# A third product of a Strassen-Winograd gate-and-up stage divided once more, with its results assembled in PSUM banks, in a GEGLU kernel on one core

## The chip, the core and the metric

The kernel runs on one core of a Trainium2 chip. Its engines work side by side, each through a queue of its own in program order: TensorE (PE: matmuls, and PEld: the loads of their stationary operand), VectorE (DVE), ScalarE (ACT), GpSimd (POOL), and SyncE (SP), which here only issues DMAs. They wait for each other by semaphores. The metric is the device time of one execution in microseconds (us), the median of several runs.

## The reference

```python
B, S, Dm, Df = 1, 2048, 1024, 3584          # x, w_gate, w_up, w_down in bfloat16
g = einsum("bsd,df->bsf", x, w_gate)
u = einsum("bsd,df->bsf", x, w_up)
h = gelu(g) * u                              # tanh form
return einsum("bsf,fd->bsd", h, w_down)
```

Here 2048 tokens with 1024 features go through two matrices to 3584 hidden features, one half passes a GELU and is multiplied by the other, and a third matrix leads back to 1024.

## The kernel before

**Winograd's form.** Each of the three matrix products is done by Strassen's method in Winograd's form: both factors are cut into quarters, a few sums of quarters are made (S1 to S4 of the weights, T1 to T4 of the inputs), and seven products of half the size, P1 to P7, take the place of eight. For gate and up, one *unit* (of 14, NU) is 256 columns of w_gate and w_up; the inputs come in two halves of 1024 tokens, p = 0 and 1, and a product of one half is four matmuls of 128x128 by 128x512. Units 0 to 3 run first, one half of the tokens at a time (`unit`, line 241). Units 4 to 13 run with both halves together (`joint`, line 299): four products P1 (raw weights, bf16), P6 = S2 T2, P5 = S1 T1, P2 (raw, bf16) and P7 = S3 T3 with four matmuls for each half and each of gate and up. Two of the seven products are divided once more there, P3 = S4 B22 (T named "tb") and P4 = A22 T4: such a product of 16 matmuls is itself done in Winograd's form, by seven half products of two matmuls each (`half`, line 295), 14 in all.

**PSUM.** There are eight banks of 128x512 float32. A unit has four banks E[p][i] (half p; i = 0 gate, 1 up), in which P1, P6 and P5 are added up one on the other, and four banks F, of which z and y hold the parts of the divided products and two the raw P2. At the end of a unit E and F change places. Intermediate states are copied out of the banks by ACT (`snap`, line 104: p1, u2, v, zz) and added by DVE (`dve`, line 88); GELU is ACT's, and `times` (line 205) makes the product h = gelu(g) u on DVE and has SP store it in DRAM (hd).

**Sums.** POOL makes the sums of weights (`sums_s`, line 163: S1 to S4 from 128x512 operands) for the next unit, the quarter sums of the divided products (`split_sums`, line 191: four operations of 128x256), the sums of the down weights (`keep_whole`, line 425: three operations of 128x512 for each of 14 chunks j, two such chunks in most units from 5 on), which SP stores in DRAM (td, line 432) for the down products, and, once, the differences of the inputs for the divided products (`split_b`, line 282: eight operations each for "tb" and "t4", lines 994 and 998, at the end of unit 3). T of the first half of the tokens lies in 20 slots, T of the second in rooms that later hold h.

**Slots.** Most small tiles share one pool of 54 slots of 2 KB a partition (kpool, line 64). A tile gets a slot that is free or will be; its first writer then waits for the last reader of the tile that was there. Sums of down weights had a pool of their own (mpool: 6 KB, one buffer), as had the products h on their way out (spool: 4 buffers of 1 KB).

**Order.** PE, DVE, POOL and SP run in the order in which the program names their instructions (line 58), ACT too in this stage (line 944). In `joint` the order is that of its statements; sums, loads and stores are asked for at seven places in it, by name ("p6", "p5", "p3", "p2", "p7", "p4", "end"; `joint_work`, line 885). The last product of a unit is finished during the next one (`rest`, line 395).

**Down products.** After unit 13, `down` (line 625) computes the output for each half of the tokens, from h and from the stored sums of down weights, which it loads again (`load12`, line 438). `inner_product` (line 578) belongs to the last half.

Of the kernel before, what the change touches and what calls it, by code (L numbers as in the profile page):

```python
# [10 lines left out]
def kernel(  # L11
# [35 lines left out]
    JOINT = 4  # L47
    H, Q, R2 = NJ // 2, N // 2, range(2)
    SLOTS = 54
# [10 lines left out]
    mpool = ctx.enter_context(tc.tile_pool(name="m", bufs=1))  # L60
# [4 lines left out]
    spool = ctx.enter_context(tc.tile_pool(name="s", bufs=4))  # L65
# [125 lines left out]
    def split_sums(a):  # L191
        a11, a12, a21, a22 = quarters(a)
        s12, s34 = [slot([P, 2, 2, P], f32r, "s") for _ in range(2)]
        pool(s12[:, 0], a21, a22, ADD)
        pool(s12[:, 1], s12[:, 0], a11, SUB)
        pool(s34[:, 0], a11, a21, SUB)
        pool(s34[:, 1], a12, s12[:, 1], SUB)
        return s12[:, 0], s12[:, 1], s34[:, 0], s34[:, 1]
# [6 lines left out]
    def times(p, fb, c, g, u):  # L205
        if (p, fb // 2) == (0, NU - 1) and h[1][c] is not None:
            dve(h[1][c][:, fb % NJ], g, u, MUL)
            return
        last = fb // 2 == NU - 1
        st = slot([P, N], bf16, "h") if last else spool.tile([P, N], bf16, name="h")  # L210
        dve(st, g, u, MUL)
        nc.sync.dma_start(out=hd[p, fb // NJ, c][:, fb % NJ], in_=st)  # L212
# [81 lines left out]

    def half(ps, lhs, rhs, fresh=False):
        for k in range(2):
            matmul(ps, lhs[:, k], rhs[k], fresh and k == 0, k == 1)

    def joint(u, E, F, todo, c21):
        GU = range(2)  # L300
        w, s = ws[u], ss[u]

        def copied(ps, *args):
            half(ps, *args)
            return snap(ps, "zz")

        def onto(t, ps):
            dve(t, ps, t, ADD)

        def gelu_of(t):  # L310
            nc.scalar.activation(t, t, ACT.Gelu_apprx_tanh)
            return t

        p1, u2, v = [[[None, None], [None, None]] for _ in range(3)]
        spread = (0, 1), (1, 0), (0, 0), (1, 1)
        for n, (p, i) in enumerate(spread):
            product(E[p][i], w[i][0][:, :, :P], XT[p, 0][:KH], True)
            p1[p][i] = snap(E[p][i], "p1")
            c21(n)
        todo("p6")  # L320
        s2 = s.pop("s2")
        for n, (p, i) in enumerate(spread):
            product(E[p][i], s2[i], T[p]["t2"], False)
            u2[p][i] = snap(E[p][i], "u2")
            c21(4 + n)
        todo("p5")
        z, y = F[0]
        s1 = s.pop("s1")
        a11, a12, a21, a22 = quarters(s["s4"])
        n1, n2, n3, n4 = ns["tb"]  # L330
        q1, q2, q3, q4 = sums.pop((u, "tb"))
        for p in range(2):
            for i in GU:
                product(E[p][i], s1[i], T[p]["t1"], False)
                v[p][i] = snap(E[p][i], "v")
            if p == 0:
                z1 = copied(z, a11, T[0]["tb"][:2], True)
                for i in GU:
                    nc.scalar.copy(out=F[1][i], in_=p1[1][i])
        todo("p3")  # L340
        z6 = copied(z, q2, n2)
        half(E[0][0], a12, T[0]["tb"][2:])
        half(y, q1, n1, True)
        onto(z1, E[0][0])
        half(E[0][1], a22, n4)
        onto(z6, y)
        z7 = copied(z, q3, n3)
        half(E[1][0], q4, T[1]["tb"][2:])
        ga = gelu_of(z1)
        onto(z6, E[1][0])  # L350
        dve(E[0][1], E[0][1], z7, ADD)
        onto(z7, y)
        times(0, 2 * u, 1, ga, E[0][1])
        dve(E[1][1], E[1][1], z7, ADD)
        gb = gelu_of(z6)
        todo("p2")
        for i in GU:
            product(F[1][i], w[i][1][:, :, :P], XT[1, 0][KH:], False)
        times(1, 2 * u, 1, gb, E[1][1])
        raw_second(F[0], 0, w)  # L360
        hb = gelu(F[1][0])
        onto(p1[0][0], F[0][0])
        dve(F[0][1], F[0][1], p1[0][1], ADD)
        times(1, 2 * u, 0, hb, F[1][1])
        ha = gelu_of(p1[0][0])
        todo("p7")
        s3 = s.pop("s3")
        n1, n2, n3, n4 = ns["t4"]
        q1, q2, q3, q4 = sums.pop((u, "t4"))
        sg, sh = sums.pop((u, "sa"))  # L370
        for i in GU:
            product(E[0][i], s3[i], T[0]["t3"], True)
        times(0, 2 * u, 0, ha, F[0][1])
        z1 = copied(z, sg[:, :2], T[0]["t4"][:2], True)
        for i in GU:
            product(E[1][i], s3[i], T[1]["t3"], True)
        onto(v[0][0], E[0][0])
        dve(F[1][0], E[0][1], v[0][1], ADD)
        onto(v[1][0], E[1][0])
        dve(F[1][1], E[1][1], v[1][1], ADD)  # L380
        todo("p4")
        z6 = copied(z, q2, n2)
        half(y, q1, n1, True)
        y5 = snap(y, "zz")
        ha = gelu_of(v[0][0])
        half(E[0][0], sg[:, 2:], T[0]["t4"][2:])
        half(E[0][1], sh, n4)
        z7 = copied(z, q3, n3)
        half(E[1][0], q4, T[1]["t4"][2:])
        hb = gelu_of(v[1][0])  # L390
        times(0, 2 * u + 1, 1, ha, F[1][0])
        times(1, 2 * u + 1, 1, hb, F[1][1])
        todo("end")

        def rest(part):
            if part == 0:
                dve(E[0][0], E[0][0], u2[0][0], ADD)
                onto(z1, E[0][0])
                for a in (u2[0][1], z7):
                    dve(E[0][1], E[0][1], a, ADD)  # L400
                for a in (u2[1][0], y5):
                    dve(E[1][0], E[1][0], a, ADD)
                onto(z6, E[1][0])
            if part == 3:
                times(0, 2 * u + 1, 0, gelu_of(z1), E[0][1])
                for a in (u2[1][1], z7, y5):
                    dve(E[1][1], E[1][1], a, ADD)
            if part == 7:
                times(1, 2 * u + 1, 0, gelu_of(z6), E[1][1])

        return rest
# [13 lines left out]
    def keep_whole(j):  # L425
        ra, rb = wraw.pop(j)
        m = made[j] = mpool.tile([P, 3, N], f32r, name="m")
        pool(m[:, 0], ra[:, N:], ra[:, :N], SUB)
        pool(m[:, 1], rb[:, N:], m[:, 0], SUB)
        pool(m[:, 2], rb[:, :N], m[:, 1], SUB)  # L430

    def store_made(j):
        nc.sync.dma_start(out=td[:, j], in_=made[j][:, :3].bitcast(f32))
# [138 lines left out]
    def store(ip, c, i, dc, put):  # L572
        st = slot([P, N], bf16, "st") if (c, dc) == (1, 0) else spool.tile([P, N], bf16, name="h")
        put(st)
        r0 = (2 * ip + c) * N + i * P
        nc.sync.dma_start(out=out2[r0 : r0 + P, dc * N : (dc + 1) * N], in_=st)

    def inner_product(ip, e, c, ss):
        zz = [mpool.tile([P, 3, N], f32, name="m")[:, :2], wpool.tile([P, 2, N], f32, name="w")]
# [238 lines left out]
    order = ["t2"] * KH + ["t1"] * KH + ["tb"] * KH + ["n"] * 2 + ["t3"] * KH + ["t4"] * KH + ["n"] * 6  # L818
# [8 lines left out]
    def more_room():  # L827
        extra = wpool.tile([P, KH, N], f32r, name="w")
        spots["n"][2:2] = [extra[:, k] for k in range(KH)]
# [23 lines left out]
    def at_p5(n):  # L853
# [19 lines left out]
        elif n == 6:  # L873
            new_s(JOINT, "s3", "s4")

    keeps = {}
    for j in range(NJ):
        n = 3 + j
        keeps[JOINT + n // 2, ("p2", "p3")[n % 2]] = j

# [4 lines left out]
    def joint_work(u, what):  # L885
        if what == "p6":
            if u in (JOINT, JOINT + 1):
                load_next(u + 1)
            if (u, "p3") in keeps:
                fetch_wd(keeps[u, "p3"])  # L890
            if u > JOINT:
                new_s(u, "s3")
        if what == "p5":
            if (u, "p2") in keeps:
                keep_whole(keeps[u, "p2"])
            sums[u, "t4"] = split_sums([loaded(u)[i][1][:, :, P:] for i in range(2)])
        if what == "p3" and (u, "p2") in keeps:
            store_made(keeps[u, "p2"])
        if what == "p2":
            if (u, "p3") in keeps:  # L900
                keep_whole(keeps[u, "p3"])
            halves = sums_s(loaded(u), pool)["how"]
            sums[u, "sa"] = halves["sg"](None), halves["sh"](None)
            if u + 1 < NU:
                new_s(u + 1, "s1", "s2")
        if what == "p7":
            if (u, "p3") in keeps:
                store_made(keeps[u, "p3"])
            ws.pop(u)
            if u % 2 == 0 and u > JOINT:  # L910
                load_next(u + 2)
            if u + 1 < NU:
                new_s(u + 1, "s4")
# [157 lines left out]
```

## Time and profile before

| what | us |
|---|---|
| median of 3 runs (lowest, highest) | 532.36 (532.31, 532.40) |
| the profiled execution | 532.63 |
| its span, first to last instruction | 530.8 |
| units 4 to 13, PE's first matmul of unit 4 to the first of the down products | 108.98 to 352.69 |
| one joint unit | 24.3 |
| the two down products | 352.69 to 530.8 |

The page's first part gives the busy time of each engine as a share of the span. The second cuts the span in 40 slices of 13.3 us, each digit the busy share of one engine in tenths. The windows view gives the same for chosen stretches. The chain of waits starts from the last instruction and goes back to whatever released each piece of work. The timeline lists instructions in order of time; several of one kind in a row are one line, marked xN.

### The profile page before, as it was taken

Reading aid. Unit: us, or ns where it says so; the run is one execution under the profiler, and the core shown is the slowest. Engines: PE = TensorE matmul, PEld = TensorE weight load, DVE = VectorE, ACT = ScalarE, POOL = GpSimd, SP = SyncE. Lnnn points to the kernel's source line nnn. Section 1 sums busy time; section 2 is a strip of 40 time slices with the busy share of each in tenths; the row PEclk is TensorE's granted clock in tenths of the full one; section 3 lists DMA queues with packets and bytes.
Section 4 is the critical chain, followed back from the end, with each engine's and each line's share of the span. In section 5 each row is a group of like instructions: output and inputs, shape, how many; then the busy total and the mean of one; then the engine's idle time right before and its main releaser. Section 6 shows DMA issues by size and latency. Waiting matters only on the chain.

```text
span 530.8 us, 7711 instructions
## 1 busy us (share of the span) xinstructions
PE 524.2 (99%) x2380; PEld 373.5 (70%) x2411; DVE 367.5 (69%) x568; ACT 274.9 (52%) x497; POOL 306.0 (58%) x311
## 2 busy tenths in 40 slices
PE   9999999999999999999999999999999999999997
PEld 5568686876767677777777676764688885488887
DVE  2984636427687878787876878788599336768933
ACT  2555655555857585666768576832126501133340
POOL 1179899899986999799779799200000000000495
PEclk9999999999999999999999999999999999999999
DMA  9687541331346754574738453699986999982851
GB/s 247 158 190 154 126 129 49 110 109 41 106 159 195 223 191 163 205 228 143 252 127 253 160 159 118 193 389 413 382 267 205 384 411 380 395 276 87 260 159 61
DMA packets 103513, 109.57 MB, mean 206 GB/s; under 512 B 19376, under 2 KB 84656, under 8 KB 103472
## 3 DMA queue, kind: packets, MB, share of 16 engines
q1 hardware_dynamic: 103472, 109.08, 63.4%
q8 instruction: 19, 0.31, 0.2%
q14 instruction: 22, 0.18, 0.1%
HBM read 76.28 MB, written 29.62 MB: 200 GB/s over the span
## 4 chain that ended last, share of the span: by engine, by line
PE 90%; POOL 6%; DMA 2%; issue 1%; SPq 0%; DVE 0%; POOLq 0%; DVEq 0%
PE bank L110 90%; POOL h L92 3%; POOL s L92 2%; DMA w<-in_w_up_dram 1%; POOL w L92 1%; DMA xn<-in_x_dram 1%; SPq L723 0%; DVE h L89 0%; DVE st L89 0%; PE bank L730 0%; SPq L131 0%; SPq L212 0%; POOLq L92 0%; DVEq L89 0%
## 5 line engine op out<-in xcount | busy, mean ns | idle before, releaser
L110 PE MATMUL bank<-h,s 128*128 128x512 f32 x508 | 127.7, 390 | 0.2 <-POOL s L92 0.2
L92 POOL TENSOR_TENSOR q<-q 128x256 fp32r<-128x256 f32 x28 | 25.5, 943 | 164.3 <-DMA q<-td 163.7
L110 PEld LDWEIGHTS bank<-h,s 128*128 128x128 f32 x508 | 95.2, 188 | 20.8 <-POOL s L92 0.6
L110 PE MATMUL bank<-xT,w 128*128 128x512 bf16 (+1 forms) x448 | 101.0, 375 | 1.5
L92 POOL TENSOR_TENSOR s<-w 128x512 fp32r<-128x512 bf16 (+1 forms) x82 | 85.1, 1055 | 12.4 <-DMA w<-in_w_gate_dram 11.8
L110 PEld LDWEIGHTS <-w 128*128 128x128 bf16 x504 | 47.3, 98 | 58.5 <-issue 5.8
L110 PE MATMUL bank<-t,s 128*128 128x512 f32 x312 | 83.1, 406 | 0.0
L89 DVE TENSOR_TENSOR zz<-bank,zz 128x512 f32<-128x512 f32 x60 | 40.5, 689 | 41.9 <-PE bank L110 28.5
L110 PEld LDWEIGHTS bank<-t,s 128*128 128x128 f32 x312 | 57.9, 188 | 15.6 <-ACT u L106 2.3
L110 PE MATMUL bank<-q 128*128 128x512 f32 x272 | 66.9, 390 | 0.0
L110 PEld LDWEIGHTS bank<-q 128*128 128x128 f32 x272 | 51.1, 188 | 10.7
L106 ACT COPY zz<-bank 128x512 f32<-128x512 f32 x70 | 40.5, 592 | 33.8 <-PE bank L110 29.9
L106 ACT COPY p<-bank 128x512 f32<-128x512 f32 x76 | 43.6, 588 | 20.3 <-PE bank L110 20.0
L89 DVE TENSOR_TENSOR q<-h,h 128x512 fp32r<-128x512 bf16 x56 | 38.3, 683 | 15.2 <-DMA h<-hd 12.4
L106 ACT COPY u<-bank 128x512 f32<-128x512 f32 x62 | 35.8, 589 | 23.5 <-PE bank L110 23.5
L89 DVE TENSOR_TENSOR bank<-bank,zz 128x512 f32<-128x512 f32 x60 | 41.8, 697 | 1.4
L92 POOL TENSOR_TENSOR s<-s,w 128x512 fp32r<-128x512 f32 (+1 forms) x40 | 41.2, 1046 | 0.8
L92 POOL TENSOR_TENSOR s<-w,s 128x512 fp32r<-128x512 bf16 (+1 forms) x40 | 41.4, 1051 | 0.0
L110 PEld LDWEIGHTS <-h 128*128 128x128 bf16 x224 | 21.7, 98 | 26.7 <-issue 0.5
L101 ACT CAST tb<-raw 128x512 fp32r<-128x512 bf16 x28 | 17.4, 627 | 44.4 <-PE bank L110 21.1
L110 PE MATMUL bank<-raw,h 128*128 128x512 bf16 x156 | 34.8, 379 | 0.2
L92 POOL TENSOR_TENSOR m<-raw,m 128x512 fp32r<-128x512 bf16 x28 | 32.9, 1175 | 2.2
(102 smaller groups left out, 772.6 us busy)
## 6 DMA issues: line engine op xcount, KB each, us to landing
raw<-in_w_down_dram SPq DMA_DIRECT2D x72, 256.0 KB, 4.3
q<-td SPq DMA_DIRECT2D x68, 256.0 KB, 5.3
hd<-h SPq DMA_DIRECT2D x110, 128.0 KB, 1.7
td<-m SPq DMA_DIRECT2D x14, 768.0 KB, 3.4
h<-hd SPq DMA_DIRECT2D x18, 512.0 KB, 6.9
h<-hd SPq DMA_DIRECT2D x6, 768.0 KB, 8.5
w<-in_w_gate_dram SPq DMA_DIRECT2D x8, 512.0 KB, 5.3
w<-in_w_up_dram SPq DMA_DIRECT2D x8, 512.0 KB, 6.5
```

The lines of the kernel that those rows point to most:

```text
L89: nc.vector.tensor_tensor(out=out, in0=a, in1=b, op=op)
L92: nc.gpsimd.tensor_tensor(out=out, in0=a, in1=b, op=op)
L101: nc.scalar.copy(out=t, in_=src)
L106: nc.scalar.copy(out=t, in_=ps)
L110: nc.tensor.matmul(ps, lhsT=lhs, rhs=rhs, start=start, stop=stop, skip_group_check=True)
```

## The change

In units 5 to 13 the product S3 T3 is divided too, by the same seven half products, H1 to H7 in the new code; unit 4 keeps it whole. Its results are not added up from copies in SBUF: three copies on ACT (e00, e10, e01) put the common part of z into banks E, on which the remaining half products are then accumulated, and two additions on DVE (e11, e10y) add the part y5. So the sum v + S3 T3 of the up half stays in SBUF (v01, v11), and its product with the GELU (m22a, m22b) reads two tiles in SBUF, where it read one in SBUF and one bank.

The statements of `joint` become named steps (`joint_ops`), and one table, SEQUENCE, gives their order for every engine: P, X, H, K, S, G are steps on PE; a leading minus marks steps that finish the unit before; @ marks places where sums, loads and stores are asked for. Half products of "tb" are X1 to X7, those of "t4" K1 to K7, the raw P2 of the two halves S0, S1 and G0, G1.

POOL makes the quarter sums of S3 in addition, in two parts of two operations, as now for "tb" and "t4" too. The differences of T3 are made by DVE (three), POOL (three, in unit 4, and two in unit 5); those of T4 are made by DVE in unit 4, no longer by POOL at the end of unit 3. S3 of unit 4 is made within that unit.

The pools for the sums of down weights and for the products h are gone, and the slots are 59. The sums of one j are three tiles stored by three DMAs. Their units are listed in KEEPS: one j in units 5, 6, 8, 10 and 12, two in 7, 9 and 11, three in 13; those of j = 4, 5, 6, made in unit 13, stay in their slots for the down products and two thirds of them are not loaded again.

```diff
+    DIVIDED7 = 5
+    STAY = 4, 5, 6
+    KEEPS = [(u, n) for u in range(5, 14) for n in range({7: 2, 9: 2, 11: 2, 13: 3}.get(u, 1))]
-    SLOTS = 54
+    SLOTS = 59
...
-    def split_sums(a):
+    def split_sums(a, part, before=None):
         a11, a12, a21, a22 = quarters(a)
...
+        t = slot([P, 2, 2, P], f32r, "s")
+        if part == 0:
+            pool(t[:, 0], a21, a22, ADD)
+            pool(t[:, 1], t[:, 0], a11, SUB)
+        else:
+            pool(t[:, 0], a11, a21, SUB)
+            pool(t[:, 1], a12, before[1], SUB)
+        return t[:, 0], t[:, 1]
...
+    def split_b3(part, eng=pool):
+        n = ns.setdefault("t3", [[], [], [], []])
+        for k in range(2):
+            b11, b12, b21, b22 = [T[p]["t3"][h + k] for h in (0, 2) for p in range(2)]
+            if part == k:
+                n1, n2, n4 = [slot([P, N], f32r, "n") for _ in range(3)]
+                eng(n1, b12, b11, SUB)
+                eng(n2, b22, n1, SUB)
+                eng(n4, b21, n2, SUB)
...
+            if part == 2:
+                eng(b12, b22, b12, SUB)
...
+    SEQUENCE = (
+        "@start -a00u P100 -a10u P101 @tb.0 -a00z P111 -m22a p101 @tb.1 -a01u P110 p100 -v11+ "
+        "-g21a P601 -a01z @keep p110 P600 -a11u -hb2 X1 u201 -m21a P610 u200 -m22b xz1 X5 -a10y "
+        "P501 p111 -a10z @s3 u210 X6 -a11z @store P500 v01 -a11y xz6 S0 -g21b x6y X7 @t3.0 v00 "
+        "-m21b P510 sg c11a xz7 X2 X4 v10 @t3.1 P611 x00 f0 x01 ha H1 @t4.0 X3 u211 x7y S1 ga x10 "
+        "@s1 H5 e00 m12a P511 @free gb c11b y5 H6 m11a H2 v11 K1 @t4.1 e10 x11 G0 kz1 v00+ H7 f1 "
+        "H3 m12b K6 @late e01 @s2 e11 G1 ha2 e10y kz6 H4 K5 v10+ sh K2 hb v01+ @s4 K7 ky5 K3 m11b "
+        "K4 kz7 @end "
+    ).split()
...
+        def inner(letter, left, tname, z, y):
...
+                out, a, b = [
+                    (z, a11, b11), (E[0][0], a12, b21), (E[1][0], q4, b22), (E[0][1], a22, n4),
+                    (y, q1, n1), (z, q2, n2), (z, q3, n3),
+                ][n - 1]
+                half(out, a, b, n in (1, 5))
...
+        if u < DIVIDED7:
+            for name in ("H1", "H5", "H6", "H7", "e00", "e10", "e01", "y5", "e11", "e10y"):
+                ops[name] = lambda: None
+            for name, outs in (("H2", PI[:1]), ("H3", PI[2:3]), ("H4", PI[1::2])):
+                whole(name, *outs, lhs="s3", tname="t3", start=True)
+        else:
+            inner("H", quarters_of("s3"), "t3", z, y)
+            seed("e00", E[0][0], z)
+            seed("e10", E[1][0], z)
+            seed("e01", E[0][1], z)
+            copy("y5", y)
+            ops["e11"] = lambda: dve(E[1][1], z, t["y5"], ADD)
+            plus("e10y", E[1][0], "y5")
+        for p, i in PI:
+            onto(("-" if p and i else "") + f"v{p}{i}+", f"v{p}{i}", E[p][i])
...
+        multiply("-m22a", 0, 1, 1, "v00", "v01")
+        multiply("-m22b", 1, 1, 1, "v10", "v11")
...
+        m = made[j] = [slot([P, N], f32r, "m") for _ in range(3)]
...
+        for n, m in enumerate(made.pop(j)):
+            nc.sync.dma_start(out=td[:, j, n], in_=m.bitcast(f32))
...
         elif n == 6:
-            new_s(JOINT, "s3", "s4")
+            new_s(JOINT, "s4")
...
+        elif what == "keep":
+            made(keep_whole, 0)
+            if u == JOINT:
+                split_b3(0, dve)
+                split_b3(1)
+                ns["t4"] = split_b("t4", dve, place_n)
+        elif what == "store":
+            made(store_made, 0)
+            made(fetch_wd, 2)
+        elif what == "s3":
+            new_s(u, "s3")
+            if u == JOINT + 1:
+                split_b3(2)
...
+        elif name == "t3":
+            half_sums(u, "t4" if u == JOINT else name, part)
+            if more and part == 1:
+                made(keep_whole, 1)
...
+        elif what == "late":
+            made(store_made, 1)
+            if (u + 1, 0) in keeps:
+                fetch_wd(keeps[u + 1, 0])
+        elif what == "end":
+            made(store_made, 2)
             load_next(u + 2)
...
-                    if n == len(items) - 1:
-                        ns["t4"] = split_b("t4", pool, place_n)
...
+            now = joint_ops(u, E, F)
+            for name in SEQUENCE:
+                if name[0] == "@":
+                    side_work(u, name[1:])
+                elif name[0] != "-":
+                    now[name]()
+                elif last:
+                    last[name]()
+            last = now
             E, F = F, E
```

More of the change, by code (lines that the diff above doesn't have):

```diff
@@ L208, in times @@
             return
[L209 to L210 removed]
+        st = slot([P, N], bf16, "h")
         dve(st, g, u, MUL)
@@ L297, in half @@
             matmul(ps, lhs[:, k], rhs[k], fresh and k == 0, k == 1)
[L299 to L411, printed above, removed]
@@ L883, in load_next @@
             ws[u] = load_w(u, u % 2 == 1)
-    def joint_work(u, what):
-        if what == "p6":
-            if u in (JOINT, JOINT + 1):
-                load_next(u + 1)
-            if (u, "p3") in keeps:
-                fetch_wd(keeps[u, "p3"])
-            if u > JOINT:
[L892 to L913, printed above, removed]
-                sums[u + 1, "tb"] = split_sums(ss[u + 1]["s4"])
-        if what == "end" and u % 2:
@@ L916, in joint_work @@
             load_next(u + 2)
-        if what == "end" and (u + 1, "p2") in keeps:
-            fetch_wd(keeps[u + 1, "p2"])
+        if not more:
+            last_loads(what)
     turns = [(c, ko) for ko in range(NKB) for c in (1, 0)]
```

177 lines of the change are left out of this document (140 added, 37 removed).

## The prediction

> **What bounds the kernel now.** I read, in this order: the page's busy shares, the table of windows for the joint stage, the list of waits, and the chain of waits that ended last, with the timeline beside it.
>
> ```profile
> PE 524.2 (99%) x2380; PEld 373.5 (70%) x2411; DVE 367.5 (69%) x568; ACT 274.9 (52%) x497; POOL 306.0 (58%) x311
> ...
> POOL 1179899899986999799779799200000000000495
> ```
>
> TensorE is busy 99% of the span, so time goes only if matmuls go, and comes back as soon as one waits. POOL is at 58% over the span, but at 70 to 99% of each slice up to about 330 us, that is, as long as units run.
>
> ```profile
> 98.00:123.40 25.40, 25.26 (x112) 19.01 (x113) 8.77 (x14) 15.00 (x27) 25.09 (x23) 1.00 0.25 72
> ...
> 172.18:196.53 24.35, 24.23 (x106) 17.14 (x108) 19.22 (x31) 16.64 (x32) 22.93 (x26) 1.00 0.69 219
> ...
> 366.90:452.40 85.50, 85.36 (x380) 62.44 (x382) 55.49 (x89) 25.22 (x47) 0.00 (x0) 1.00 0.95 343
> ```
>
> The columns are stretch, length, then busy time of PE, PEld, DVE, ACT, POOL, and clock, DMA share, GB/s. The joint units start at 108.98 us in the timeline and follow every 24.3 us until 352.69. In one of them DVE has 5.1 us free, ACT 7.7 us, POOL 1.4 to 4.5 us. In the stretch where unit 4 begins, POOL has 0.3 us free in 25.4: there it is nearly the bound, as the chain says too:
>
> ```profile
> 120.35 5.03 POOL h L92 x4
> ...
> 129.95 0.69 POOL s L92
> ...
> 130.68 4.15 PE bank L110 x17
> ```
>
> From 98 to 130.6 us the chain runs through POOL, and PE then waits 0.20 us for it. The granted clock is 1.00 in all stretches.
>
> **The paces.** From the PE timeline: twelve float32 starts from 275.20 to 277.92 are 0.2267 us each; fifteen bf16 matmuls from 269.67 take 3.40, with 0.38 for one, so 0.2157 between starts. An old unit has 32 bf16 and 76 float32 matmuls: 32 x 0.2157 + 76 x 0.2267 = 24.13. The period is 24.34, so 0.21 is lost. Of that 0.12 is P5's first product, waiting for the copy u (eight starts from 286.85 to 288.78 take 1.93, not 1.81). The other 0.08 or 0.09 I put down to the two blocks of bf16, 0.04 for each change there and back.
>
> **Part by part.**
>
> *S3 T3 divided.* Sixteen matmuls become seven half products of two. Nine units lose two float32 matmuls each: 18 x 0.2267 = 4.1 us less.
>
> *The table.* Its PE steps hold five bf16 blocks in a unit (P1 together, S0, S1, G0, G1) where two stood: 3 x 0.04 x 10 = 1.2 us more. But u201 now stands seven PE steps ahead of P501, so the 0.12 in each unit goes: 1.2 less. The 0.20 at 130.68 belongs to an order that is gone: 0.2 less. So far 4.3 less.
>
> *What the new results cost.* ACT has four more copies in a unit (e00, e10, e01, y5): 35 steps at about 0.50 us between starts, 17.6 of 23.9. DVE has two more (e11, e10y): 32 at 0.60 is 19.2, with 0.12 more where a step reads what the one before it wrote, about 20.2. Both fit. I laid the table against PE's clock with these paces. The closest meetings are x7y before H5 (ends 0.84 us before it), then K4, P601, G1, H7 and X7 at 0.86 to 0.88: no PE step waits, and each has 0.8 us in hand. Cover gone, each late step costs PE what it is late beyond that.
>
> *POOL in units 5 to 13.* Eight whole sums at 1.125 (2.25 for two in the timeline) 9.0; four quarter sums each of S4, S3 (2.91) and A22 (2.64) 8.5; down weights 3.63 for one j, 11 of them in units 5 to 12, so 5.0 a unit. That is 22.5 of 23.9; before it was 20.9 of 24.3. On average it fits; units 7, 9 and 11 with two j have 24.8 and borrow about 1 us from their neighbours, which leave 2.7. Needed latest against made: H5's sums at 15.2 us into the unit, made by about 9.3. No cost.
>
> *Down weights in slots.* Three stores of 256 KB for one of 768: two more issues of 0.33 us on SP's queue for each j. They wait behind POOL's last sum only; behind them stand stores of h, and SP already waits 13.3 us at the longest with no engine late. The first loads of h for the down products are freed by P511 at 16.5 us of unit 13, where they were issued 16.5 us into it (344.86): same lead. Keeping j 4 to 6 saves loads in a stretch where PE is busy 85.36 of 85.50: nothing.
>
> *The start of unit 4* is where I expect the price. POOL no longer makes the halves of T4 (eight sums, 118.98 to 129.19), but three of T3's; S3 moves behind these. From the rows: S4 101.33 to 103.58; T_B's split 10.22, to 113.80; its sums 2.91, to 116.71; three for T3 at 1.28, to 120.54; the first S3 1.13, to 121.67. H2 needs that one after 24 bf16 and 46 float32 matmuls, at 108.98 + 15.61 = 124.59: 2.9 us in hand. But DVE now makes three of T3's and all eight of T4's, eleven operations with both inputs in SBUF, and nothing stands ahead of them once its last product of unit 3 ends at 109.7. Two places show such an operation meeting POOL:
>
> ```profile
> L92 POOL TENSOR_TENSOR q<-q x28: 734/740/6431, 498.7 to 524.0; 128x256 fp32r<-128x256 f32 x28
> ```
> ```profile
> L92 POOL TENSOR_TENSOR s<-w x2: 1157/1406/1654, 11.8 to 13.6; 128x512 fp32r<-128x512 bf16 x2
> ```
>
> In the first (ns, least, median, longest) POOL's operation of 0.74 us took 6.43, and DVE ran ten such back to back from 498.41 to 504.51. In the second one of 1.157 took 1.654, beside a single DVE operation of 0.69: POOL lost 0.50 of its 0.69. By the second, eleven cost POOL 5.5 us, and H2 is 5.5 - 2.9 = 2.6 us late. By the first they cost 0.98 of 11 x 0.60 to 0.69, 6.5 to 7.4 us: 3.6 to 4.5 late. If they never meet: nothing. I take 2.6, since most of the eleven read what the one before wrote and come singly, as in the second row. [...]
>
> *Steady units* have two such products (m22a, m22b), where the unit before had none: 2 x 0.5 to 0.7 of POOL's time, 23.5 to 23.9 of 23.9. Just covered; bounds 0 and, at 0.2 over, 2 us in all; I take 0.
>
> **Sum.** The profiled execution took 532.63, 1.8 outside its span. 532.63 - 4.3 + 2.6 = 530.9; the median is 0.27 lower, so 530.7.
>
> **Rivals.** *Nothing meets in unit 4* (chance 0.28): DVE and POOL overlap as other rows of them do. Then 528.1. For it: all steps have 0.8 us in hand. Against: the two rows.
>
> *The whole of each operation is lost in unit 4* (0.12), as in the first row: 528.1 + 4.5 = 532.6. For it: that row is the cleaner of the two. Against: DVE's ten came back to back there, and the eleven mostly don't.
>
> *Slots run short* (0.12): a slot is written again only after its last reader. Lifetimes from the table add up to about 29 slots on average, and 26 more are held (20 sums of T for the first half, six of T3's): 55 of 59, near 60 at 12 us into a unit. Before, ACT's copies waited five times for POOL in units 5 to 13 (1.7 us the longest), which I read as slots, and PE didn't see it. If each unit loses 0.5, 10 x 0.5 = 5: 533.1.
>
> *POOL's runs keep DVE out* (0.18): this is the slow side. If a run of POOL operations without a gap holds what DVE's operation needs, as DVE's run held it at 498.7, then m22b, due 4.9 us into a unit, waits for the end of S3's run at 7.8 or later. Behind it stand a10y and a10z, which free the bank that S0 writes at 9.35; they end at 6.9. So from a wait of 2.4 us on PE pays; here 0.5 to 1.7 in each of nine units, and the entry pays 4.5 or more: 528.1 + 4.5 + 4.5 to 15 = 537 to 548, about 540. Against it: POOL's chained sums leave gaps (0.1 us at 107.2 and 112.2) in which DVE may start.
>
> **How the numbers follow.** Forecast 530.7 with chance 0.30, its own range 529 to 532 (a lateness of 1 to 4). With 528.1 at 0.28, 532.6 at 0.12, 533.1 at 0.12 and about 540 at 0.18, eight in ten lie between 527.7 and 537. A measurement of this kernel tells 0.2%, about 1.1 us, from no change: 531.3 to 533.4 is the same. Faster: 0.28, 0.23 of the forecast and 0.02 of the slots: 0.53. Same: 0.07 of the forecast, 0.08 of the whole loss and 0.05 of the slots: 0.20. Slower: 0.04 of the whole loss, 0.05 of the slots and the 0.18: 0.27.
>
> **What would show it.** In the windows, units 5 to 13 at 23.9 us; 24.3 or more refutes the count or shows a wait in each. In the timeline of POOL from 109 to 125 us, sums of T_B longer than 1.30 and the first S3 after 124.6 show the meeting; PE then waits for POOL between X5 and H2. DVE's m22b begun over a microsecond after its turn is the slow rival. ACT copies waiting for POOL or a DMA, and PE for them, are the slots. I am wrong altogether if PE waits where none of these stands.

## The result, and the profile after

The changed kernel takes 537.27 us (median of 4 runs, 536.28 to 537.89) against 532.38 (4 runs, 532.31 to 532.72) for the kernel before on the same chip: a ratio of 1.0089, 95% interval 1.0071 to 1.0106. It is slower by 0.9%. The profiled execution took 536.89, its span 535.1 (530.8 before).

The page of the changed kernel has the lines that answer to those shown of before:

```profile
PE 523.2 (98%) x2362; PEld 369.9 (69%) x2393; DVE 398.1 (74%) x597; ACT 290.9 (54%) x533; POOL 338.0 (63%) x344
...
POOL 1169999999999989999999999940000000000394
PEclk9999999998999999999999999999999999999999
```

TensorE's share fell from 99 to 98%: matmuls went, but TensorE stood still as well. POOL has hardly a slice under 9 until the units end, and in the tenth slice the granted clock shows an 8 that the kernel before does not have. The windows say where (columns as before: stretch, length, busy time of PE, PEld, DVE, ACT, POOL, clock, DMA share, GB/s). Unit 4 of the kernel before:

```profile
108.98:133.58 24.60, 24.33 (x106) 16.93 (x107) 11.07 (x18) 15.01 (x28) 24.21 (x24) 1.00 0.26 76
```

The changed kernel:

```profile
109.07:139.93 30.86, 26.24 (x106) 17.90 (x107) 26.82 (x29) 15.24 (x28) 30.31 (x28) 0.94 0.25 78
139.93:163.86 23.93, 23.82 (x105) 16.62 (x106) 20.73 (x33) 18.62 (x35) 22.63 (x24) 1.00 0.44 138
331.64:356.86 25.22, 23.99 (x106) 16.65 (x107) 22.65 (x36) 18.52 (x35) 21.46 (x23) 1.00 0.88 285
125.57:128.98 3.41, 0.30 (x1) 0.30 (x2) 3.37 (x7) 1.98 (x4) 3.33 (x4) 1.00 0.00 0
128.98:132.39 3.41, 3.41 (x9) 2.67 (x8) 3.09 (x6) 1.40 (x3) 3.41 (x5) 0.50 0.15 49
```

The first row is unit 4: 30.86 us, where it took 24.60. The second is a divided unit: 23.93, where it took 24.34; all from 5 to 12 are like it but unit 7 (24.18). The third is unit 13 with the seam to the down products: 25.22. The last two lie within unit 4: a stretch of 3.41 us with PE nearly idle, and the next 3.41 us at half the clock. So the span's 4.3 us are +6.3 in unit 4, about -3.1 in units 5 to 12, +0.9 in unit 13, and 0.2 elsewhere. This is the profiled execution. The mean clock listed for the four runs is 0.997 in three, which is what one such stretch makes of 535 us, and 1.000 in the shortest (536.28): the drop is not in every execution, and the kernel is slower without it too.

PE's timeline in unit 4 has two waits, in brackets with what ended them:

```profile
116.70 0.50 PE L111 MATMUL bank<-h,s 128*128 128x512 f32 x1 [1.03 <-POOL s L93]
...
128.68 1.84 PE L111 MATMUL bank<-h,s 128*128 128x512 f32 x4 [3.53 <-ACT u L107]
```

The first is X5, waiting for sums of T_B. The second is P511, waiting for the copy u211, which empties its bank. The copy itself takes 0.56 us; the chain of waits tells what it stood behind:

```profile
116.10 4.54 DVE h L90 x4
120.67 2.31 DVE h L90 x2
...
123.96 1.76 DVE h L90
125.72 0.60 DVE xz L90
126.32 0.61 DVE p L90
127.00 0.59 ACT bank L335
...
128.68 12.51 PE bank L111 x47
```

It runs through VectorE, not through POOL. The differences on DVE (h<-h and the like, L90) end at 125.6. Only then come x6y (xz) and c11a (p); c11a empties the bank that ACT's step f0 (L335) fills, and ACT had stood 4.39 us for it. In ACT's queue ha and u211 stood behind f0. VectorE's own rows show the size:

```profile
109.70 1.28 DVE L90 TENSOR_TENSOR n<-h,t 128x512 fp32r<-128x512 f32 x1
...
112.70 1.67 DVE L90 TENSOR_TENSOR n<-t,n 128x512 fp32r<-128x512 f32 x1
114.29 1.78 DVE L90 TENSOR_TENSOR w<-h,t 128x512 fp32r<-128x512 f32 x1
...
118.27 1.22 DVE L90 TENSOR_TENSOR h<-t,h 128x512 fp32r<-128x512 f32 x1
...
125.64 0.68 DVE L90 TENSOR_TENSOR xz<-bank,xz 128x512 f32<-128x512 f32 x1
```

An addition that reads a bank takes 0.68; the eleven that read two tiles in SBUF take 1.10 to 1.78 and end after 15.9 us, not 7. POOL's timeline in the same stretch has 1.60 to 1.74 for what takes it 1.28 to 1.30 where nothing meets it, and 1.17 for 0.74:

```profile
107.91 1.30 POOL L93 TENSOR_TENSOR h<-tb,h 128x512 fp32r<-128x512 f32 x1
...
112.08 1.74 POOL L93 TENSOR_TENSOR h<-h 128x512 fp32r<-128x512 f32 x1
```

Their starts alternate, one operation each: VectorE's at 111.09, 112.70 and 114.29, POOL's at 110.52, 112.08 and 113.78. VectorE's take 0.88 to 1.09 more than 0.69 there, most of the length of one of POOL's (1.28), and POOL's 0.32 to 0.46 more, about half of one of VectorE's or a little more. POOL's first sum of S3, behind all this, is late as well:

```profile
125.13 1.60 POOL L93 TENSOR_TENSOR s<-w 128x512 fp32r<-128x512 bf16 x1
```

The seam is in SP's timeline. Seven loads of h, which the first down products read, go out at 351.66; ahead of them six loads of down weights (L528) took 6.74 us, 3.5 of it waiting for a slot whose last reader was the store of a product issued just ahead, at 343.85. PE waited 1.12 and 0.29 us for h.

```profile
344.36 6.74 SPq L528 DMA_DIRECT2D raw<-in_w_down_dram  x6
351.19 0.42 SPq L214 DMA_DIRECT2D hd<-h  x1
351.66 4.58 SPq L608 DMA_DIRECT2D h<-hd  x7
```

### The profile page after: what moved, and what is told of

The parts are those of the page before. It is cut to its first block, busy times and chain, and to the rows that moved or that the text cites. A ratio compares the mean times of both kernels' runs of the same rounds, so it can differ in the third digit from the quotient of the medians.

```text
span 535.1 us, 7968 instructions
## 1 busy us (share of the span) xinstructions
PE 523.2 (98%) x2362; PEld 369.9 (69%) x2393; DVE 398.1 (74%) x597; ACT 290.9 (54%) x533; POOL 338.0 (63%) x344
## 4 chain that ended last, share of the span: by engine, by line
PE 90%; SPq 4%; DVE 3%; DMA 2%; issue 1%; ACT 0%; DVEq 0%; ACTq 0%
PE bank L111 90%; SPq L779 2%; DVE h L90 2%; DMA h<-hd 1%; DVE n L90 1%; SPq L785 1%; DMA x<-in_x_dram 0%; SPq L132 0%; DVE w L90 0%; SPq L765 0%; DVE st L90 0%; DVE p L90 0%; DVE xz L90 0%; ACT bank L335 0%; ACT p L344 0%
## 5 line engine op out<-in xcount | busy, mean ns | idle before, releaser
L111 PE MATMUL bank<-xT,w 128*128 128x512 bf16 (+1 forms) x448 | 107.8, 376 | 1.3
L111 PEld LDWEIGHTS bank<-h,s 128*128 128x128 f32 x472 | 88.8, 188 | 26.4 <-ACT u L107 4.0
L111 PEld LDWEIGHTS <-w 128*128 128x128 bf16 x504 | 45.0, 98 | 59.4 <-issue 14.1
L111 PE MATMUL bank<-t,s 128*128 128x512 f32 x276 | 74.6, 402 | 0.0
L111 PE MATMUL bank<-q 128*128 128x512 f32 x248 | 61.5, 390 | 0.0
L111 PEld LDWEIGHTS bank<-t,s 128*128 128x128 f32 x276 | 52.4, 190 | 12.1
L90 DVE TENSOR_TENSOR q<-h,h 128x512 fp32r<-128x512 bf16 x56 | 38.3, 685 | 21.3 <-DMA h<-hd 21.3
L111 PEld LDWEIGHTS bank<-q 128*128 128x128 f32 x248 | 46.5, 188 | 9.8
L93 POOL TENSOR_TENSOR s<-s,s 128x256 fp32r<-128x256 f32 x57 | 43.3, 786 | 1.9 <-PE bank L111 0.2
L90 DVE TENSOR_TENSOR xz<-bank,xz 128x512 f32<-128x512 f32 x40 | 27.5, 690 | 15.9 <-PE bank L111 7.4
L90 DVE TENSOR_TENSOR h<-g,bank 128x512 bf16<-128x512 f32 x42 | 28.6, 684 | 6.4 <-ACT g L205 3.5
```

Source lines behind the costliest of these rows:

```text
L90: nc.vector.tensor_tensor(out=out, in0=a, in1=b, op=op)
L93: nc.gpsimd.tensor_tensor(out=out, in0=a, in1=b, op=op)
L111: nc.tensor.matmul(ps, lhsT=lhs, rhs=rhs, start=start, stop=stop, skip_group_check=True)
```

## The experiments

**Theory.** VectorE's eleven differences, with both operands in SBUF, and POOL's work hold each other up (1.10 to 1.78 us in place of 0.69, 1.60 to 1.74 in place of 1.28, above); VectorE is 7.2 us late for x6y (it begins 16.57 us into unit 4, against 9.38 in e1_one_input and 9.40 in e2_left_out, below), and ACT's order hands this to PE. By this theory, with one operand in a bank (e1_one_input) or without the eleven (e2_left_out), unit 4 takes 24.4 to 24.8 us again and the kernel 537.3 - 6.2 = 531 (530 to 532). **Rivals.** The new table costs the time by itself (its order of steps, its bank use); or the eleven are simply too many for VectorE's queue there, wherever they read from. Times in brackets are the lowest and highest run; the kernel before took 532.42 to 532.76 in all four groups of runs.

**e1_one_input.** The same eleven operations at the same places, one operand from a bank; what they compute is then not the differences that the products need.

```diff
-                split_b3(0, dve)
+                def from_bank(out, a, b, op):
+                    dve(out, F[1][0], b, op)
+
+                split_b3(0, from_bank)
                 split_b3(1)
-                ns["t4"] = split_b("t4", dve, place_n)
+                ns["t4"] = split_b("t4", from_bank, place_n)
```

> The changed kernel, with one edit: the eleven operations that DVE makes at the start of unit 4 (three differences of T3, eight of T4) read one operand from a PSUM bank (f0, free at that time) instead of from SBUF. Their number, size and place are unchanged; the values of T4's and some of T3's differences are not the right ones. [...] Rival, the table (unit 4 is late because the table's order does not suit it, whatever DVE's operations read): unit 4 stays above 29 us, time 536 to 538. Rival, the queue (eleven operations ahead of DVE's first addition are too many at any length): something between, 533 to 536.

Measured: 530.71 (530.33 to 531.96), ratio 0.9964 (0.9952 to 0.9976). Two rows of VectorE's timeline, one of the eleven and x6y:

```profile
112.97 0.69 DVE L90 TENSOR_TENSOR h<-bank,w 128x512 fp32r<-128x512 f32 x1
...
118.66 0.69 DVE L90 TENSOR_TENSOR xz<-bank,xz 128x512 f32<-128x512 f32 x1 [1.28 <-ACT xz L107]
```

Each takes 0.68 or 0.69, POOL's beside them 1.27 to 1.30 again; unit 4 takes 24.38, with no wait and the clock at 1.0; x6y waits for ACT, not for the eleven. The table and the number of operations are the same as in the changed kernel, so neither costs the 6 us: the second operand in SBUF does: beside POOL, an operation takes 1.10 to 1.78 us with it and 0.68 or 0.69 without.

**e2_left_out.** The eleven are not issued at all.

```diff
-            if part == k:
+            if part == 0 and k == 0:
+                for i, b in ((0, b12), (1, b22), (3, b21)):
+                    n[i].append(b)
+            elif part == k:
...
-                split_b3(0, dve)
+                split_b3(0)
                 split_b3(1)
-                ns["t4"] = split_b("t4", dve, place_n)
+                ns["t4"] = [
+                    [T[p]["t4"][h + k] for k in range(2)]
+                    for h, p in ((0, 1), (2, 1), (0, 1), (2, 0))
+                ]
```

> The changed kernel without those eleven operations of DVE: the half products read T3 and T4 themselves in place of these differences, so that part of the computation is left out. [...] Queue: clearly faster than with one operand from PSUM, by 2 us or more. Table: 536 to 538.

Measured: 528.65 (528.41 to 529.54), ratio 0.9932 (0.9915 to 0.9948). The windows of unit 4:

```profile
108.71:133.10 24.39, 24.39 (x110) 17.02 (x109) 11.43 (x19) 15.25 (x28) 23.92 (x25) 1.00 0.33 98
```

That is as long as in e1, so VectorE has room for eleven operations of 0.68. By the median alone, 2.06 below e1, this is what the rival of the queue had named; the place decides against it, since nothing of it lies in unit 4. What lies between the two profiled executions (530.73 and 528.41) is elsewhere: 1.07 in unit 13 with the seam (25.01 against 23.94), 0.48 in unit 7, 0.11 in unit 11, 0.57 ahead of unit 4. This kernel holds three slots less, which points to slots but does not show it.

**e3_seam.** Three loads of down weights go out behind the loads of h.

```diff
-        ... "t4.0": range(8, 11), "s1": range(11, NJ)}.get(what, ()):
+        ... "t4.0": range(8, 11), "late": range(11, NJ)}.get(what, ()):
```

> The changed kernel with one edit: the last three loads of the down weights' chunks (n = 11 to 13) are asked for at @late instead of at @s1 of unit 13, behind the loads of h in SP's order. Theory of SP's order (the first of these three waited 3.5 us for a slot whose store had not landed, and the loads of h stood behind it): the loads of h are issued about 348 instead of 351.7, PE's waits of 1.1 and 0.3 us for them at the start of the down products go, time 537.3 - 1.4 = 535.9. Rival, bandwidth (the DMA engines are full at that point, so h lands no earlier): the waits stay, 537.3.

Measured: 537.45 (535.81 to 540.39), ratio 1.0097 (1.0062 to 1.0133). In its profile unit 13 is 23.94 and PE does not wait at the seam, as expected. The median shows nothing of it. The stretch at half the clock in unit 4 lasts 6.83 us here, 3.41 in the profile of the changed kernel, and the clocks listed for the four runs (0.993 to 0.997) are lower than the changed kernel's too; but the times do not go by the clocks (535.81 at 0.993, 540.39 at 0.994), so what scatters them stays open. By time alone the run decides nothing; e8_both repeats it without that stretch.

**e4_whole7.** P7 stays whole in all units (`DIVIDED7 = 14`); two of T3's tiles of the second half of the tokens are still overwritten in unit 5, so P7 reads changed values from unit 6 on.

> The changed kernel with S3 T3 left whole in all units (the table, the slots and the sums of POOL and DVE for it unchanged). Theory of the count: units 5 to 13 take 24.3 us instead of 23.93, nine times 0.40, time 537.3 + 3.7 = 541. Rival (part of the shorter unit comes from the table's other order, not from the division): units at 24.1 to 24.2, 539 to 540. Rival (the division itself costs elsewhere, in slots or on ACT): no more than 538.

Measured: 539.62 (538.46 to 540.21), ratio 1.0129 (1.0114 to 1.0145). All units from 5 to 13 take 24.39, and unit 4 31.97 (the clock listed for this execution is 0.993). The table alone thus gains nothing against the 24.34 of before; it costs 0.05. The division gives 24.39 - 23.93 = 0.46 a unit, two float32 matmuls at 0.2267.

**e5_u211.** The copy u211 stands ahead of f0 in the table.

```diff
-        ... P611 x00 f0 x01 ha H1 @t4.0 X3 u211 x7y S1 ga x10 "
+        ... P611 u211 x00 f0 x01 ha H1 @t4.0 X3 x7y S1 ga x10 "
```

> The changed kernel with one step of the table moved: the copy u211 stands at the head of ScalarE's four steps x00's partner f0, ha, u211, ahead of f0 instead of behind ha. Nothing else is changed. In the profile of the changed kernel PE stood 3.53 us ahead of P511 in unit 4 for this copy, which stood in ScalarE's queue behind the copy f0 (bank<-p), which waited 4.39 us for VectorE's c11a; c11a was late because of the eleven differences on VectorE. By the theory that the lateness of VectorE reaches PE through ScalarE's order, the one wait of 3.53 us goes and a later wait for VectorE's own results (x00, x7y or c11a, which are due a little later) takes part of it; no single idle stretch is then over 3 us, the clock keeps 1.0 in units 4 and 5 and the time is 534 to 536. The meeting of VectorE and GpSimd itself is untouched: VectorE's differences still take 1.1 to 1.8 us. By the rival, that the order in ScalarE's queue does not matter and PE only waits for VectorE at another place, the same 3.5 us and the same clock of 0.5 are seen, and the time stays at 537.

Measured: 537.44 (536.14 to 538.46), ratio 1.0084 (1.0066 to 1.0103): no gain. The long wait did go; PE's timeline has a shorter one in its place, and the windows show the clock:

```profile
127.28 1.17 PE L111 MATMUL bank<-t,s 128*128 128x512 f32 x4 [1.55 <-DVE xz L90]
```
```profile
125.43:128.84 3.41, 1.79 (x7) 0.97 (x6) 3.38 (x6) 1.68 (x3) 3.33 (x5) 1.00 0.00 0
128.84:132.25 3.41, 3.41 (x9) 1.82 (x8) 3.31 (x7) 2.18 (x4) 3.41 (x5) 0.50 0.22 73
```

Unit 4 is 29.2 us, 1.6 less than in the changed kernel. But in this execution the clock halved all the same, which I had expected to go with the long wait; that it takes an idle stretch of 3 us, as I had reckoned, no run shows, and here PE was busy 1.79 of the 3.41 us ahead. At the seam PE waited 2.64 us for h, after which it halved once more (357.53 to 360.94). Two of the four runs list a clock of 0.999 and 1.000, so there it did stay up; they took 536.68 and 536.14, about as much as the changed kernel's one run at 1.000 (536.28). So the expected 534 to 536 was missed with the drop and without it. ACT's order carries the lateness to PE but is not its cause: put right, VectorE's own results are late next.

**e6_before_dve.** The kernel before with VectorE making T4's eight differences.

```diff
-                        ns["t4"] = split_b("t4", pool, place_n)
+                        ns["t4"] = split_b("t4", dve, place_n)
```

> The kernel before with one part of the change alone: the eight differences of T4 are made by VectorE instead of by GpSimd, at the place they had (behind the last whole block, ahead of unit 4). T3 is not divided and the order of steps is that of before. By the theory of the shared operand reads, the eight (1.28 us each on GpSimd, 0.69 on VectorE where nothing meets them) take 1.1 to 1.8 us on VectorE while GpSimd makes the differences and sums of T_B, so they end near 122 us instead of 116, VectorE's first sum of unit 4 (121.19 before) is 1 us or so late, GpSimd's sums of T_B are 2 to 4 us late for z6, and the time is 533 to 536, although GpSimd is spared 10 us and its wait of 0.2 at 130.68 goes. By the rival, that two engines on separate operands do not hold each other and only the new table loses, it is 532.4 to 532.7.

Measured: 532.98 (532.49 to 533.99), ratio 1.0008 (0.9996 to 1.0019): the same. VectorE's timeline shows that the meeting is there in full:

```profile
113.16 1.78 DVE L89 TENSOR_TENSOR h<-h 128x512 fp32r<-128x512 f32 x1
...
121.72 1.27 DVE L89 TENSOR_TENSOR zz<-bank,zz 128x512 f32<-128x512 f32 x2
```

The eight take 1.11 to 1.78 and end at 121.7. In the kernel before VectorE's first sum of unit 4 comes at 121.19, so they make it 0.5 late (0.3 counted from the start of the unit), and the steps behind have that in hand. POOL is also spared eight differences here, so what the run shows is that the move as a whole costs nothing. My expectation of 533 to 536 priced the meeting and not the due time. In the changed kernel eleven end at 125.6, with a sum due at about 118.5.

**e7_spread.** A kernel with all parts of the change, its differences placed by these findings: VectorE makes four of T4's, which fit ahead of 118; POOL the other four, late; T3 is divided from unit 6 on, its differences on POOL in unit 5; the three loads stand as in e3_seam.

```diff
+    DIVIDED7 = 6
+    KEEPS = [(u, n) for u in range(6, 14) for n in range({7: 2, 8: 2, 9: 2, 11: 2, 13: 3}.get(u, 1))]
...
             eng(n1, b12, b11, SUB)
             eng(n2, b22, n1, SUB)
-            eng(b12, b22, b12, SUB)
-            eng(n4, b21, n2, SUB)
+            def rest(b12=b12, b22=b22, n4=n4, b21=b21, n2=n2):
+                (then or eng)(b12, b22, b12, SUB)
+                (then or eng)(n4, b21, n2, SUB)
...
+                        half_sums(JOINT, "tb", 0)
                         ns["tb"] = split_b("tb", pool, place_n)
-                        half_sums(JOINT, "tb", 0), half_sums(JOINT, "tb", 1)
+                        half_sums(JOINT, "tb", 1)
```

> The changed kernel with all of its parts, and the differences placed otherwise. T3 is divided from unit 6 on instead of unit 5, its eight differences all on GpSimd in unit 5, which makes no down weights for it (those of unit 5 go to unit 8). Of T4's eight differences VectorE makes the four that come first (they end before its first sum of unit 4 is due at 118), GpSimd the four that are due last, behind its sums for T4. The first two sums for T_B stand ahead of T_B's differences. The loads of down weights 11 to 13 stand behind the products m12b, so that no product waits for their slots at the seam. By the theory (VectorE's differences beside GpSimd's take 1.6 us each, the loss is lateness at the due steps, and the seam's 1.1 us are slots): unit 4 takes 24.4 us, eight units 23.94, no wait at the seam, the clock stays 1.0, and the time is 528.9 to 530.5, faster than before by 0.4 to 0.7%. By the rival, that the division's own gain is lost elsewhere (bank order, table), it is not under 531.5.

Measured: 535.32 (535.03 to 538.68), ratio 1.0060 (1.0041 to 1.0080). Unit 4 is right: 24.16, the four at 1.27 to 1.79, no wait. The time is not: units 5, 7, 8 and 9 take 26.68, 25.01, 24.64 and 25.47. PE waits there for copies on ACT, and ACT for a slot; in unit 5 the row in ACT's timeline is

```profile
148.23 0.59 ACT L107 COPY v<-bank 128x512 f32<-128x512 f32 x1 [3.27 <-POOL s L93]
```

The copy's slot was last read by a sum of S3, which stood behind six differences of T3 in POOL's queue.

**e8_both.** The edits of e1_one_input and e3_seam together.

> As e1_one_input (VectorE's eleven differences read one operand from a bank, so their values are not right), and the loads of down weights 11 to 13 moved behind the products m12b as in e3_seam. By the theory that the seam's wait is a matter of slots and of SP's order, worth 1.1 us, and that its gain in e3_seam was hidden by the length of the clock's drop: 529.3 to 530.0, against 530.71 of e1_one_input, with unit 13 at 23.9 us instead of 25.0. By the rival, that the loads that are moved are then late for the down products: 530.7 or more.

Measured: 529.19 (528.43 to 530.34), ratio 0.9939 (0.9926 to 0.9952), 1.5 below e1. The median is 0.1 under the 529.3 to 530.0 that the theory gave. The profiled execution is the longest of the six (530.34); in it unit 13 is 23.93, but PE waits 0.93 for h two microseconds further on, so the seam is not always free.

**e9_seven and e10_six.** e7_spread with less for POOL at once: T3 divided from unit 7 (e9) or 6 (e10), its differences spread over units 5 to 7 or 5 and 6, the down weights otherwise.

```diff
-    DIVIDED7 = 6
+    DIVIDED7 = 7
+    KEEPS = [(5, 1)] + [(u, n) for u in range(6, 14) for n in range({6: 2, 9: 2, 11: 2, 13: 3}.get(u, 1))]
...
             if u == JOINT + 1:
                 split_b3(0)
-                split_b3(1)
...
+            if u == JOINT + 2:
+                split_b3(1)
```

In e10 DIVIDED7 stays 6, the list has `{7: 2, 9: 2, 11: 2, 13: 3}`, and split_b3(1) comes late in unit 5.

> As e7_spread, with T3 divided from unit 7 on (seven units instead of nine), T3's differences on GpSimd three in unit 5, three in unit 6 and two in unit 7, and the down weights made as 1 in unit 5, 2 in unit 6, 1 each in 7 and 8, from unit 9 on as in the changed kernel. In e7_spread unit 4 took 24.16, and the loss had moved to units 5 and 7 to 9, where ScalarE's copies waited 1.4 to 3.3 us for a slot (its last reader a sum of S3 on GpSimd, late behind six differences of T3, or a store of a product queued on SP behind a load that waited for GpSimd). By the theory that these are slots held up by GpSimd being late: with no unit in which GpSimd has over 23.4 of work, units 4 to 6 take 24.2 to 24.4, units 7 to 13 23.94, and the time is 532.4 - 7 x 0.4 - 0.2 = 529.4 (528.9 to 530.2). By the rival, that the 59 slots are too few whatever GpSimd does: waits of 0.5 us or more for ScalarE in two units or more, and 531 to 533.

> As e9_seven, but T3 divided from unit 6 on, its differences on GpSimd three early and three late in unit 5 and two in unit 6, with one down weight made in unit 5 (late in it), one in unit 6, and from unit 7 on as in the changed kernel. GpSimd has 23.4 of work in unit 5 and 22.5 in unit 7. By the theory of slots held up by a late GpSimd: unit 5 without a wait over 0.5, a wait of 0.2 to 0.8 left in unit 7 as in e8_both, and 529.2 to 530.2. By the rival of too few slots: 531 to 533.

Measured: e9 532.28 (530.88 to 533.18), ratio 0.9986 (0.9975 to 0.9996); e10 536.98 (535.54 to 538.32), ratio 1.0074 (1.0059 to 1.0088). Unit 4 is 24.4 in both, without a wait. Neither came out by the theory (e9 lies in the range of its rival, too few slots; e10 beyond both): in e9 unit 9 takes 25.48, unit 7 24.6; in e10 units 6 and 7 take 26.5 and 27.1. Each time ACT's copy xz waits for a slot, mostly one whose last reader is a difference of down weights on POOL ("POOL m": 2.7 us at the longest in e9, 4.3 in e10). I read this as a POOL that comes late out of units 4 and 5 and has no idle time in which to catch up.

**e11_slots57.** e8_both with `SLOTS = 57` in place of 59.

> As e8_both (one operand of the eleven from a bank, values not right; loads 11 to 13 moved), with 57 common slots instead of 59 and nothing else changed: GpSimd has the same work. In e8_both the only wait left on PE over 0.5 us was 0.77 in unit 7. By the theory that the waits of ScalarE's copies in units 6 to 9 (e7_spread, e9_seven, e10_six) are a shortage of slots, two slots fewer bring such waits back: PE waits of 0.5 to 2 us for ScalarE's copies in two units or more, ended by a reader on GpSimd or a store of a product, and the time is 530.5 to 533 against 529.2. By the rival, that those waits come from GpSimd being late alone, and the number of slots has room: 529.0 to 529.7.

Measured: 540.34 (539.89 to 543.83), ratio 1.0169 (1.0143 to 1.0196): 11 us for two slots, far more than the 530.5 to 533 that the theory gave. Units 7, 8, 10 and 12 take 25.0 to 26.7, with POOL's work unchanged. The list of ACT's waits (total, times, longest) has

```profile
ACT xz L107 <- POOL m L93: 13.7, 6, 4.0
```

So at 59 next to none is spare, and a delay of a reader shows.

**e12_later.** e9_seven with the down weights `{8: 2, 10: 2, 12: 2, 13: 3}`.

> As e9_seven, with the down weights made 1 each in units 5, 6, 7, 9 and 11, 2 each in 8, 10 and 12 and 3 in 13 (e9_seven: 2 in 6, 9 and 11). In e9_seven GpSimd came 3 us late out of units 4 to 6 and had no idle time to make it good, and PE waited 0.23, 0.50, 1.55 and 0.16 us in units 6, 7, 9 and 11 and 0.4 at the seam, mostly for ScalarE's copies whose slots a down weight's differences on GpSimd still held. By the theory that a late GpSimd holds the slots: with lighter units 6 and 7 GpSimd is early again in unit 8, and 530.0 to 531.3. By the rival, that it only moves the same waits to units 8 to 12: 532 to 533.

Measured: 532.13 (531.08 to 532.93), ratio 0.9989 (0.9980 to 0.9998). Units 4 to 7 now run as they should (24.4 three times, 23.93), and 0.5 to 0.8 is lost in units 8, 10 and 13 each: the rival's number. With e9_seven it is the fastest of the kernels that leave nothing out, both ahead of the kernel before by 0.1%, at the edge of what can be measured. What e8 shows to be possible, 529.2, was not reached by one.

## Why the prediction was wrong

It gave 530.7 (527.7 to 537.0), with 0.53 for faster; the time is 537.27, slower. Point by point, by its steps:

1. *S3 T3 divided, and the table*: right. 23.9 a unit was forecast, 23.93 is measured; e4 gives 0.46 for the division alone and next to nothing for the table (0.05 more).
2. *ACT and DVE fit*: right for steady units. VectorE is busy 20.7 of 23.9 in unit 5, and no step waits there.
3. *POOL at 22.5 of 23.9 in units 5 to 13*: right on average (22.6 in unit 5), and with no cost as long as nothing makes POOL late. What e7 to e12 add is that the rest is too small to recover in.
4. *The start of unit 4* is the step that failed. The prediction saw the meeting, but from one side: it priced what POOL loses to the eleven (5.5 us) and let VectorE keep its 0.69. Its two rows had shown no more: in both VectorE had begun first (498.41 before POOL's 498.69, 11.78 before 11.83) and kept 0.68 or 0.69. In unit 4 an operation of POOL was under way (109.16) when VectorE's first came (109.70). POOL's side was about the right size: its first sum of S3 ended at 126.73, 2.1 after the 124.59 at which H2 was to read it, where 2.6 was forecast; PE paid 1.03 of POOL's lateness at X5, and at 126.73 it already stood at P511. VectorE lost more, 15.9 us for the eleven instead of 7, and it had a step due at about 118.5. "All steps have 0.8 us in hand" held for a VectorE on time. The whole-loss rival used the same one-sided sum.
5. What follows from VectorE's lateness was not in the sum at all: through ACT's in-order queue to P511, 3.53 us, and then, in this execution, half the clock for 3.41 us, about 1.7 us of work. With X5's 1.03 this is 6.3 us, what unit 4 is longer. The prediction's last sign, PE waiting where none of its rivals stands, is this wait. What takes the place of the 1.7 in the run without the drop was not profiled.
6. *Down weights in slots, same lead*: wrong. The lead was compared by the last reader of h's room alone; SP's queue ahead of the loads of h held loads that waited 3.5 us for a slot. Cost 1.3 in the changed kernel (unit 13 takes 25.22, in e3 23.94) and 1.1 without the meeting (25.01 in e1, 23.93 in e8).
7. *Steady units' two products m22a, m22b at nothing*: right for the time of seven units. From unit 5 on they take 0.68 to 1.71 us, 1.14 in the middle, where POOL is at work, and PE's units stay at 23.93; the two that fall behind POOL's last work (after 353.9 us) take 0.68 with the same two inputs in SBUF. In unit 7, where they take most (1.71 and 1.28), part of the 0.25 of point 8 may be theirs; that is not shown.
8. *Slots run short* was a rival at 0.12, 0.5 a unit. In the changed kernel it cost 0.25 in unit 7, where a copy of ACT waits 1.68 us for the store of a product, and the seam; e11 shows how near it was: two slots fewer, 11 us. *POOL's runs keep DVE out* gave the right sign for the wrong place: not m22b in nine units, but VectorE's differences in one.

The sum with the measured sizes: 530.8 (span before) - 3.1 + 6.3 + 0.9 + 0.2 = 535.1. That the time lies only 0.3 outside the range is luck: the range reached to 537.0 for other rivals, and its middle was worked out without this path.

What stays open: how far the waits in units 6 to 10 of e9 and e12 are slots and how far POOL's lateness, since each brings on the other; and what a VectorE that reads one of the operands from a bank would cost with right values, that is with copies into banks ahead of it, which was not tried.

## What to carry to other kernels

Moving work from a full engine to an idle one pays only if the two don't hold each other: look at the operands first (here VectorE's operations with two SBUF inputs beside a busy GpSimd took 1.10 to 1.78 us in place of 0.69, and GpSimd's 1.60 to 1.74 in place of 1.28), and charge the meeting to both sides. Then follow the slower engine to its first due step and through every in-order queue behind it; eight such operations were free where about 12 us lay ahead of the due step (e6), and eleven cost 6 where there were about 9. And where tiles share slots, a late reader is a late writer somewhere else, so count what is free at the worst moment, not on average.

## What the runs showed of the hardware

**The clock went down after stretches in which PE was not idle throughout.** The drops to 0.50 lasted 3.41 us (from 128.98 in the changed kernel, from 128.84 and 357.53 in e5) or 6.83 (from 127.11 in e3). The two starts in e5 lie 228.69 us apart, 67 times 3.41 within the rounding, as if the clock changed at fixed steps of that length; one pair does not prove it. In the 3.41 us just ahead of a drop PE was busy 0.30 us (changed kernel), 1.79 and 0.77 (e5), 1.15 (e3). In e7 two stretches of that length with PE busy 2.68 and 2.25 (144.36 to 151.18) were followed by none, and neither was one in e11 (216.15 to 219.56) with 1.65, less than the 1.79 ahead of a drop in e5. So the busy time of these 3.41 us alone does not tell when the clock goes down; what does is not shown.

**Two engines taking turns.** Two outcomes are on record. In the kernel before one operation of POOL stood 6.43 us from 498.69 while ten of VectorE's ran at 0.68 or 0.69 each; in unit 4 of the changed kernel the starts alternate, and both are slowed (1.10 to 1.78 us for VectorE's, 1.60 to 1.74 for POOL's of 1.28). What decides between the two, and by what means one holds the other, is not shown. One after the other, POOL's 1.28 and VectorE's 0.69 would make a pair 1.97; where both are 128x512, pairs start 1.56 to 1.82 us apart in unit 4 (from 110.52 to 116.10 and from 120.04 on), so 0.15 to 0.4 of each pair overlaps.
